# Streaming every product's moving operand as two interleaved halves, with the output put back in order on the host

## Chip, cores and metric

The kernel runs on one core of one Trainium2 chip. The metric is the device time of one execution in microseconds (us). Before the change it is 2234.18 us, the median of three runs that lie between 2234.03 and 2234.66 us.

## What is computed

A causal mixing over 7 tokens with softmaxed taps (one set of taps for each of 8 heads of 24 channels), and behind it a two-layer MLP with a squared ReLU. 8 x 4096 = 32768 tokens (S is 4096) of 192 channels each; the hidden layer has 2048 units.

```
w = softmax(weight, axis=-1)                       # 8 heads x 7 taps
x_pad = zeros(6 tokens) ++ x                       # per batch of 4096 tokens
attn[b, s, h*24:(h+1)*24] = sum_k w[h, k] * x_pad[b, s + k, h*24:(h+1)*24]
h = attn.reshape(32768, 192) @ w_in                # 192 -> 2048
r = maximum(h, 0)
out = (s * r * r + b) @ w_out                      # 2048 -> 192
```

## The kernel before, in words

**Layout.** Everything is kept transposed: channels or hidden units lie on the partitions, tokens along the free axis. A block is BLK = 512 tokens, so there are 64 blocks; two blocks make a unit that is loaded together. The output in memory is `outT`, 192 x 32768, and the host transposes it.

**Split operands.** Products are made in float32r (4 bytes an element, read in one pass). To keep precision each operand is held as a rounded high part and a low part, and three products stand for one: high x high, low weight x high, high weight x low. `sA`, `wA`, `tB` and `wB` are the two parts of the mixed tokens (`w...` are copies with the two halves of the partitions swapped); `W` and `WB` hold the split weights; `qh` and `ql` are the two parts of the squared hidden layer.

**First layer, `first` (L522, product at L531).** For a block and a pair `p` of hidden groups (8 pairs of 2 x 128 units) it fills a PSUM tile `h` of 128 x 2 x 512 with 18 products. Each has 64 contraction rows and 512 columns of tokens. The rows of group 0 lie on partitions 0 to 63 and those of group 1 on partitions 64 to 127, so that two products, one in each half of the array, run side by side. The text calls such a couple a **slot** of TensorE.

**Between the layers.** ACT takes the ReLU (L545) and squares it (L552); DVE rounds it to `qh` (L554) and subtracts to get `ql` (L559). All of these work on 128 x 1024 elements.

**Second layer, `second` (L604, product at L614).** 20 products of 64 rows and 512 columns for each block and pair, again two side by side, accumulate into four PSUM tiles. In blocks 0 and 1 `second_whole` (L569, products at L576 to L583) does it with 10 products of the full 128 rows, each a slot of its own. `last` (L667) finishes the last pair of the last block with 10 full products (L673, L674, L686).

**Order.** In the body each step issues `first` of one pair and then `second` of the pair LAG = 2 steps back, so that the work of ACT and DVE on a pair lies beside products of others. PSUM holds two `h` tiles. The convolution of later blocks is done on DVE in pieces between the steps; in the head two blocks' convolution is done by products in full float32 (`conv_tensor`, L257), where one product in the code gives two instructions. The head also has warm-up products (L388) and two products with a negated identity (L230).

**The streamed operand.** A matmul names the output, the stationary operand (weights) and the moving operand, which is streamed through the array column by column. In all lines that the change touches the moving operand is a row of 512 adjacent float32r elements on each partition, such as `sA[j][r, 0, :]` or `qh[:, i, :]`, and the output is a row of 512 adjacent elements of one PSUM bank.

Of the kernel before, what the change touches and what calls it, by code (L numbers as in the profile page):

```python
# [17 lines left out]
P = 128  # L18
BLK = 512
# [18 lines left out]
def conv_attention_then_squared_relu_mlp(  # L38
# [23 lines left out]
    nc = tc.nc  # L62
    D, T = outT.shape
# [4 lines left out]
    NF = 2 * NPAIR  # L68
# [43 lines left out]
    def in_order(*engines):  # L112
# [4 lines left out]
        for e in engines:  # L117
            mine = [i for i in traced[start:] if i.engine == e.engine]
            for before, i in zip(mine, mine[1:]):
# [6 lines left out]
                    reason="in_order",  # L126
                )


    class Tokens:  # L130
        def __init__(self, n):
# [143 lines left out]
    def w_in(part, p, chunk, rows):  # L275
        return W[rows, p, part, chunk * P : (chunk + 1) * P]

    def w_outA(part, f, rows=slice(0, P)):
        return W[rows, f // 2, part, CI + f % 2 * P :][:, 0:P]

    def w_outB(f, rows=slice(0, P)):
        return WB[rows, f // 2, f % 2, :]
# [239 lines left out]
    def first(n, j, p, meanwhile=None):  # L522
        h = ps_h.tile([P, 2, BLK], F32, name="h")
        halves = [tok[n].half(j, i) for i in range(2)]

        def both(w, part, at, start, stop):

            for i in range(2):
                chunk = halves[i][at]
                rows = slice(i * HB, (i + 1) * HB)  # L530
                nc.tensor.matmul(  # L531
                    h[:, i, :], w_in(w, p, chunk[0], rows), chunk[part], start=start, stop=stop
                )

        for at in (0, 2, 1):
            both(0, 1, at, at == 0, False)
            both(0, 2, at, False, False)
            both(1, 1, at, False, at == 1)
            if meanwhile and at == 0:
                meanwhile()  # L540
        return h
# [22 lines left out]
    def accumulators(n, j, p):  # L564
        if p == 0:
            acc[n, j] = [ps_o.tile([P, BLK], F32, name=f"acc{k}") for k in (1, 2, 1, 2)[: 4 if n else 2]]
        return acc[n, j]

    def second_whole(n, j, p, qh, ql):  # L569


        a1, a2 = accumulators(n, j, p)
        for i in range(2):
            f = 2 * p + i
            st, sp = f == 0, f == NF - 1
            nc.tensor.matmul(a2, w_outB(f), qh[:, i, :], start=st, stop=False)  # L576
            nc.tensor.matmul(a2, w_outB(f), ql[:, i, :], start=False, stop=sp)  # L577
        for i in range(2):
            f = 2 * p + i
            st, sp = f == 0, f == NF - 1  # L580
            nc.tensor.matmul(a1, w_outA(1, f), qh[:, i, :], start=st, stop=False)  # L581
            nc.tensor.matmul(a1, w_outA(0, f), qh[:, i, :], start=False, stop=False)  # L582
            nc.tensor.matmul(a1, w_outA(0, f), ql[:, i, :], start=False, stop=sp)  # L583
        if p == NPAIR - 1:
            t0 = n * SUP + j * BLK
            oA = outs.tile([P, BLK], F32, name="oA")
            nc.vector.tensor_scalar(oA, a1, sb, None, op0=ALU.mult)
            oC = outs.tile([DB, BLK], F32, name="oC", bufs=1)
            nc.scalar.activation(oC, a2[DB:P, :], AF.Identity, scale=sb[DB:P])
            oB = outs.tile([P, BLK], F32, name="oB")[0:DB]  # L590
            nc.vector.scalar_tensor_tensor(
                oB, a2[0:DB, :], sb[0:DB], oC, op0=ALU.mult, op1=ALU.add
            )
            unbiased.append((oA, outT[0:P, t0 : t0 + BLK], 0))
            unbiased.append((oB, outT[P:D, t0 : t0 + BLK], 2))
            del acc[n, j]
# [7 lines left out]
    def second(n, j, p, qh, ql):  # L604
        if (n, j, p) == steps[-1]:
            return last(n, j, qh, ql)
        accs = accumulators(n, j, p)

        ends = [NF - 1, NF - 1 if (n, j) != steps[-1][:2] else NF - 3]

        def both(to, w, f, q, start=False, stop=False):
            for i in range(2):
                r = slice(i * HB, (i + 1) * HB)
                nc.tensor.matmul(  # L614
                    accs[to + 2 * i], w(f, r), q[r, f % 2, :],
                    start=start and f == 0, stop=stop and f == ends[i],
                )

        for f in (2 * p, 2 * p + 1):
            both(1, w_outB, f, qh, start=True)  # L620
            both(1, w_outB, f, ql, stop=True)
        for f in (2 * p, 2 * p + 1):
            both(0, loA, f, qh, start=True)
            both(0, hiA, f, qh)
            both(0, hiA, f, ql, stop=True)
        if p == NPAIR - 1:
            t0 = n * SUP + j * BLK
            early = (n, j) == (1, 0)

            o = {}  # L630
            for k, name in ((1, "oB"), (0, "oA")):
                o[k] = outs.tile([P, BLK], F32, name=name)
                o[k + 2] = outs.tile([P, BLK], F32, name=name + "2", bufs=1)
                nc.scalar.activation(
                    o[k], accs[k], AF.Identity, scale=sb, bias=0.0 if early else bias[:, k : k + 1]
                )
                nc.scalar.activation(o[k + 2], accs[k + 2], AF.Identity, scale=sb)  # L637
            nc.gpsimd.tensor_tensor(o[1], o[1], o[3], op=ALU.add)  # L638

            oC = outs.tile([DB, BLK], F32, name="oC", bufs=1)  # L640
            nc.sync.dma_start(oC, o[1][DB:P])
            nc.gpsimd.tensor_tensor(o[0], o[0], o[2], op=ALU.add)
            toA, toB = outT[0:P, t0 : t0 + BLK], outT[P:D, t0 : t0 + BLK]
            oB = o[1][0:DB] if early else oC
            if not early:
                nc.sync.dma_start(toA, o[0])
            nc.gpsimd.tensor_tensor(oB, oC, o[1][0:DB], op=ALU.add)
            if early:
                unbiased.extend(((o[0], toA, 0), (oB, toB, 2)))
            else:  # L650
                nc.sync.dma_start(toB, oB)
            del acc[n, j]

    def upper_sums(accs):

        uA = outs.tile([P, BLK], F32, name="oA2", bufs=1)
        uB = outs.tile([DB, BLK], F32, name="oC", bufs=1)
        nc.scalar.activation(
            uB, accs[3][DB:P], AF.Identity, scale=sb[DB:P], bias=bias[DB:P, 1:2]
        )  # L660
        nc.scalar.activation(uA, accs[2], AF.Identity, scale=sb, bias=bias[:, 0:1])
        nc.vector.scalar_tensor_tensor(
            uB, accs[3][0:DB], sb[0:DB], uB, op0=ALU.mult, op1=ALU.add
        )
        return uA, uB

    def last(n, j, qh, ql):  # L667

        accs = accumulators(n, j, NPAIR - 1)
        uA, uB = upper_sums(accs)  # L670
        t0 = n * SUP + j * BLK
        for f in (NF - 2, NF - 1):
            nc.tensor.matmul(accs[1], w_outB(f), qh[:, f % 2, :], start=False, stop=False)  # L673
            nc.tensor.matmul(accs[1], w_outB(f), ql[:, f % 2, :], start=False, stop=f == NF - 1)  # L674
        oB = outs.tile([P, BLK], F32, name="oB")[0:DB]
        nc.vector.scalar_tensor_tensor(  # L676
            oB, accs[1][0:DB], sb[0:DB], uB, op0=ALU.mult, op1=ALU.add
        )
        nc.vector.scalar_tensor_tensor(
            oB, accs[1][DB:P], sb[DB:P], oB, op0=ALU.mult, op1=ALU.add  # L680
        )
        nc.sync.dma_start(outT[P:D, t0 : t0 + BLK], oB)
        oA = outs.tile([P, BLK], F32, name="oA")
        for f in (NF - 2, NF - 1):
            for w, q in ((loA, qh), (hiA, qh), (hiA, ql)):
                nc.tensor.matmul(  # L686
                    accs[0], w(f, slice(0, P)), q[:, f % 2, :],
                    start=False, stop=f == NF - 1 and q is ql,
                )
        for k, e in enumerate((nc.scalar, nc.sync)):  # L690
            c = slice(k * BLK // 2, (k + 1) * BLK // 2)
            nc.vector.scalar_tensor_tensor(
                oA[:, c], accs[0][:, c], sb, uA[:, c], op0=ALU.mult, op1=ALU.add
            )
            e.dma_start(outT[0:P, t0 + c.start : t0 + c.stop], oA[:, c])
# [81 lines left out]
    for n, j, p in steps:  # L777
# [7 lines left out]
        with begun() if n == 1 else ExitStack():  # L785
            h = first(n, j, p)
# [62 lines left out]
```

## Time and profile before

| | |
|---|---|
| median of the runs | 2234.18 us |
| profiled execution, first to last instruction | 2232.1 us |
| TensorE (PE) busy | 2226.5 us, 19330 products |
| weight loads (PEld) busy | 1829.2 us |
| VectorE (DVE) busy | 1755.6 us |
| ScalarE (ACT) busy | 1284.7 us |
| GpSimd (POOL) busy | 317.2 us |
| granted TensorE clock | 1.000 |

The span is what the profiler saw between the first and the last instruction; what lies around it makes up the difference of some 2 us to the median. Products of a matmul stream overlap each other: the time of one in the profile (386 ns) is longer than the distance between starts, and busy time counts overlapped time once. So the rate of TensorE is read from how many products start in a window, not from the duration of one. Two products that lie side by side in the two halves of the array start together.

### The profile page before, as it was taken

To read this page: it belongs to the slowest core of one execution; us is meant where nothing else is said; L and a number is where in the kernel's file an instruction comes from. 1 tells how busy PE (TensorE), PEld (TensorE's weight loads), DVE (VectorE), ACT (ScalarE), POOL (GpSimd) and SP (SyncE) were. 2 spreads that over 40 slices of the span, in tenths; PEclk is the share of its full clock that TensorE was granted. 3 is DMA by queue.
4 is the path that set the end of the run, shared out by engine and by line. 5 is a ranking of instruction groups with operands and counts; after the bars stand their busy time and mean duration, and the time that the engine had idled before them with its cause. 6 is when DMAs were issued, how large, how long until landed. Compare 5 with 4: busy or idle time off the path is not lost.

```text
span 2232.1 us, 45079 instructions
## 1 busy us (share of the span) xinstructions
PE 2226.5 (100%) x19330; PEld 1829.2 (82%) x19330; DVE 1755.6 (79%) x1997; ACT 1284.7 (58%) x1408; POOL 317.2 (14%) x205
## 2 busy tenths in 40 slices
PE   9999999999999999999999999999999999999999
PEld 6788888888888888888888888888888888888887
DVE  9898778777787787777877878778777787787764
ACT  8755555655555556555555555555655555556554
POOL 0022101111111011110110111101101111011110
PEclk9999999999999999999999999999999999999999
DMA  5113112121121111211111111112121121111110
GB/s 180 39 39 91 39 44 62 51 56 44 44 58 53 53 44 46 55 53 53 44 53 49 54 53 53 49 43 62 51 55 44 44 58 53 53 44 42 45 39 17
DMA packets 46168, 117.51 MB, mean 53 GB/s; under 512 B 7760, under 2 KB 8016, under 8 KB 45968
## 3 DMA queue, kind: packets, MB, share of 16 engines
q1 hardware_dynamic: 45824, 114.50, 18.6%
q8 instruction: 151, 2.47, 0.5%
q14 instruction: 49, 0.40, 0.1%
q10 hardware_dynamic: 144, 0.13, 0.0%
HBM read 31.64 MB, written 25.17 MB: 25 GB/s over the span
## 4 chain that ended last, share of the span: by engine, by line
PE 99%; DVE 0%; ACT 0%; issue 0%; DVEq 0%; POOL 0%; POOLq 0%
PE acc L614 50%; PE h L531 47%; PE acc L257 1%; PE acc L576 0%; PE acc L577 0%; PE acc L583 0%; PE acc L582 0%; PE acc L581 0%; PE acc L388 0%; DVE ql L559 0%; DVE accA L163 0%; DVE qh L554 0%; ACT q L552 0%; ACT q L545 0%; DVE oB L676 0%; DVE tB L216 0%
## 5 line engine op out<-in xcount | busy, mean ns | idle before, releaser
L545 ACT ACTIVATE q<-h 128x1024 f32<-128x1024 f32 x512 | 525.6, 1026 | 903.4 <-PE h L531 901.1
L559 DVE TENSOR_TENSOR ql<-q,qh 128x1024 fp32r<-128x1024 f32 x512 | 657.5, 1284 | 55.2 <-ACT qh L554 2.6
L554 DVE CAST qh<-q 128x1024 fp32r<-128x1024 f32 x497 | 370.5, 745 | 396.2 <-ACT q L552 393.8
L614 PE MATMUL acc<-qh,W 64*128 64x512 f32 x3960 | 609.9, 386 | 0.0
L552 ACT ACTIVATE q<-q 128x1024 f32<-128x1024 f32 x512 | 543.5, 1061 | 16.0
L614 PEld LDWEIGHTS acc<-qh,W 64*128 64x128 f32 x3960 | 370.9, 184 | 78.0
L531 PE MATMUL h<-sA,W 64*128 64x512 f32 x3072 | 432.4, 387 | 0.0
L531 PE MATMUL h<-wA,W 64*128 64x512 f32 x3072 | 431.5, 386 | 0.0
L531 PE MATMUL h<-tB,W 64*128 64x512 f32 x1536 | 429.9, 386 | 0.0
L531 PE MATMUL h<-wB,W 64*128 64x512 f32 x1536 | 429.9, 386 | 0.0
L614 PE MATMUL acc<-ql,WB 64*128 64x512 f32 x1980 | 385.7, 386 | 0.1
L614 PE MATMUL acc<-qh,WB 64*128 64x512 f32 x1980 | 385.6, 386 | 0.0
L614 PE MATMUL acc<-ql,W 64*128 64x512 f32 x1980 | 385.4, 386 | 0.0
L638 POOL TENSOR_TENSOR oB<-oB,oB 128x512 f32<-128x512 f32 x61 | 114.9, 1884 | 1672.6 <-ACT oB L637 1672.6
L163 DVE SCALAR_TENSOR_TENSOR accA<-xA,tap,accA 128x512 f32<-128x512 f32 x378 | 340.5, 901 | 6.8
L531 PEld LDWEIGHTS h<-sA,W 64*128 64x128 f32 x3072 | 287.3, 184 | 62.9 <-issue 1.8
L531 PEld LDWEIGHTS h<-wA,W 64*128 64x128 f32 x3072 | 287.8, 184 | 60.5
L531 PEld LDWEIGHTS h<-tB,W 64*128 64x128 f32 x1536 | 282.6, 184 | 40.5 <-issue 0.2
L531 PEld LDWEIGHTS h<-wB,W 64*128 64x128 f32 x1536 | 282.5, 184 | 20.1
L614 PEld LDWEIGHTS acc<-ql,WB 64*128 64x128 f32 x1980 | 185.5, 184 | 39.7 <-DVE ql L559 0.8
L614 PEld LDWEIGHTS acc<-ql,W 64*128 64x128 f32 x1980 | 185.5, 184 | 39.0
L614 PEld LDWEIGHTS acc<-qh,WB 64*128 64x128 f32 x1980 | 185.5, 184 | 38.8
(115 smaller groups left out, 1037.2 us busy)
## 6 DMA issues: line engine op xcount, KB each, us to landing
wA<-sA SPq DMA_DIRECT2D x126, 256.0 KB, 3.6
outT<-oA SPq DMA_DIRECT2D x63, 256.0 KB, 2.0
wB<-tB SPq DMA_DIRECT2D x60, 256.0 KB, 3.4
xA<-in_xA SPq DMA_DIRECT2D x24, 515.0 KB, 3.6
xB<-in_xB SPq DMA_DIRECT2D x32, 259.0 KB, 2.6
oC<-oB SPq DMA_DIRECT2D x61, 128.0 KB, 2.2
outT<-oC SPq DMA_DIRECT2D x60, 128.0 KB, 2.3
words<-in_w SPq DMA_DIRECT2D x7, 768.0 KB, 6.4
```

The source lines that it names most:

```text
L163: nc.vector.scalar_tensor_tensor(acc, src, w[:, k : k + 1], acc, op0=ALU.mult, op1=ALU.add)
L257: nc.tensor.matmul(acc, diag[:, k, :], x[:, k : k + BLK], start=k == 0, stop=k == K - 1)
L531: nc.tensor.matmul(h[:, i, :], w_in(w, p, chunk[0], rows), chunk[part], start=start, stop=stop)
L545: nc.scalar.activation(q, h, AF.Relu)
L552: nc.scalar.activation(q, q, AF.Square)
L554: cast(qh, q)
L559: nc.vector.tensor_tensor(ql, q, qh.bitcast(F32), op=ALU.subtract)
L614: nc.tensor.matmul(accs[to + 2 * i], w(f, r), q[r, f % 2, :], start=start and f == 0, stop=stop and f == ends[i],)
L638: nc.gpsimd.tensor_tensor(o[1], o[1], o[3], op=ALU.add)
```

## The change

Each moving operand of the products in `first`, `second`, `second_whole` and `last` is passed through a view that reads its 512 columns in the order 0, 256, 1, 257, 2, 258, and so on. Nothing is copied: only the access pattern of the instruction differs, a dimension of 256 steps of one element outside and a dimension of 2 with a step of 256 elements (1024 bytes) inside. The PSUM tiles are written as before, 512 adjacent columns.

So the tokens of a block stand in interleaved order in `h`. The second layer reads `qh` and `ql`, which are in that order, through the same view again, so that column 4a + 2u + v of its output is token 256u + 128v + a of the block. ReLU, square, rounding and the scaled sums work element by element and don't depend on the order. The host puts each block's columns back in order; this is outside the device time.

The products of the head (L257, L388, L230) and the two small products for the bias keep their operands. The instructions of every engine, their tiles, shapes and order are the same before and after; only line numbers shift by four or five.

```diff
+    def folded(columns):
+
+        return columns.rearrange("p (a b) -> p b a", a=2)
...
                 nc.tensor.matmul(
-                    h[:, i, :], w_in(w, p, chunk[0], rows), chunk[part], start=start, stop=stop
+                    h[:, i, :], w_in(w, p, chunk[0], rows), folded(chunk[part]),
+                    start=start, stop=stop,
                 )
...
-            nc.tensor.matmul(a2, w_outB(f), qh[:, i, :], start=st, stop=False)
-            nc.tensor.matmul(a2, w_outB(f), ql[:, i, :], start=False, stop=sp)
+            nc.tensor.matmul(a2, w_outB(f), folded(qh[:, i, :]), start=st, stop=False)
+            nc.tensor.matmul(a2, w_outB(f), folded(ql[:, i, :]), start=False, stop=sp)
...
-            nc.tensor.matmul(a1, w_outA(1, f), qh[:, i, :], start=st, stop=False)
-            nc.tensor.matmul(a1, w_outA(0, f), qh[:, i, :], start=False, stop=False)
-            nc.tensor.matmul(a1, w_outA(0, f), ql[:, i, :], start=False, stop=sp)
+            nc.tensor.matmul(a1, w_outA(1, f), folded(qh[:, i, :]), start=st, stop=False)
+            nc.tensor.matmul(a1, w_outA(0, f), folded(qh[:, i, :]), start=False, stop=False)
+            nc.tensor.matmul(a1, w_outA(0, f), folded(ql[:, i, :]), start=False, stop=sp)
...
                 nc.tensor.matmul(
-                    accs[to + 2 * i], w(f, r), q[r, f % 2, :],
+                    accs[to + 2 * i], w(f, r), folded(q[r, f % 2, :]),
...
-            nc.tensor.matmul(accs[1], w_outB(f), qh[:, f % 2, :], start=False, stop=False)
-            nc.tensor.matmul(accs[1], w_outB(f), ql[:, f % 2, :], start=False, stop=f == NF - 1)
+            nc.tensor.matmul(accs[1], w_outB(f), folded(qh[:, f % 2, :]), start=False, stop=False)
+            nc.tensor.matmul(accs[1], w_outB(f), folded(ql[:, f % 2, :]), start=False, stop=f == NF - 1)
...
-                    accs[0], w(f, slice(0, P)), q[:, f % 2, :],
+                    accs[0], w(f, slice(0, P)), folded(q[:, f % 2, :]),
...
-    return np.ascontiguousarray(r.results[0]["outT"].T)
+    out = r.results[0]["outT"].reshape(D, T // BLK, P, 2, 2)
+    return np.ascontiguousarray(out.transpose(1, 3, 4, 2, 0)).reshape(T, D)
```

## The prediction

> **What bounds the kernel now.** First the page's busy times and its chain of waits, to see which engine sets the end.
>
> ```profile
> span 2232.1 us, 45079 instructions
> PE 2226.5 (100%) x19330; PEld 1829.2 (82%) x19330; DVE 1755.6 (79%) x1997; ACT 1284.7 (58%) x1408; POOL 317.2 (14%) x205
> PEclk9999999999999999999999999999999999999999
> PE 99%; DVE 0%; ACT 0%; issue 0%; DVEq 0%; POOL 0%; POOLq 0%
> ```
>
> 99% of the chain that ended last is TensorE (PE) itself, and its clock is granted in full throughout. A busy PE is not yet a PE at its peak, so I look next at who made it wait (the waits of PE alone) and at how many products start in a stretch (busy time by windows: one of the steady body, one from the first changed product to the last).
>
> ```profile
> PE acc L388 <- POOL xA L145: 1.0, 1, 1.0
> 1000.00:2000.00 1000.00, 1000.00 (x8826) 826.48 (x8824) 785.51 (x872) 565.01 (x609) 143.28 (x90) 1.00 0.19 50
> 17.49:2227.00 2209.51, 2209.43 (x19295) 1821.58 (x19295) 1740.64 (x1968) 1271.78 (x1378) 316.32 (x197) 1.00 0.19 51
> ```
>
> PE waited 1.0 us in the whole run, at the warm-up. In the body 8826 products start in 1000 us. They start in couples, one in each half of the array, so 4413 slots: **226.6 ns a slot** of 512 columns. The chain says the same (start, duration, line, count): 40 products, 20 slots, in 4.53 us.
>
> ```profile
> 133.36 4.53 PE acc L614 x40
> ```
>
> So PE streams back to back: about 2.26 columns per ns, each column one 4-byte element read on each partition. Nothing but the time of a slot sets the length of the program.
>
> **The change part by part.** No instruction is added, removed or moved on any engine, no wait is new, no byte more is moved; the output rows have their old shape, and the host's reordering is not device time. What changes is how a slot reads its moving operand: adjacent elements before, afterwards each element 1024 bytes away from the one read just before it. So the sum has one term: the number of slots times what a slot gains or loses. The groups of products:
>
> ```profile
> L531 PE MATMUL h<-sA,W 64*128 64x512 f32 x3072 | 432.4, 387 | 0.0
> L531 PE MATMUL h<-wA,W 64*128 64x512 f32 x3072 | 431.5, 386 | 0.0
> L531 PE MATMUL h<-tB,W 64*128 64x512 f32 x1536 | 429.9, 386 | 0.0
> L531 PE MATMUL h<-wB,W 64*128 64x512 f32 x1536 | 429.9, 386 | 0.0
> L614 PE MATMUL acc<-qh,W 64*128 64x512 f32 x3960 | 609.9, 386 | 0.0
> L614 PE MATMUL acc<-ql,WB 64*128 64x512 f32 x1980 | 385.7, 386 | 0.1
> L614 PE MATMUL acc<-qh,WB 64*128 64x512 f32 x1980 | 385.6, 386 | 0.0
> L614 PE MATMUL acc<-ql,W 64*128 64x512 f32 x1980 | 385.4, 386 | 0.0
> ...
> L576 PE MATMUL acc<-qh,WB 128*128 128x512 f32 x32 | 13.0, 407 | 0.0
> L577 PE MATMUL acc<-ql,WB 128*128 128x512 f32 x32 | 12.6, 395 | 0.0
> L583 PE MATMUL acc<-ql,W 128*128 128x512 f32 x32 | 12.5, 391 | 0.0
> L582 PE MATMUL acc<-qh,W 128*128 128x512 f32 x32 | 12.5, 390 | 0.0
> L581 PE MATMUL acc<-qh,W 128*128 128x512 f32 x32 | 12.5, 389 | 0.0
> ```
>
> L531: 9216 products, 4608 slots. L614: 9900, 4950 slots. L576 to L583: 160 full products, 160 slots. The last pair adds 10 full ones by the code (L673, L674, L686). Together **9728 slots**; at 226.6 ns they make 2204.4 us of the 2209.5 us between 17.49 and 2227.00. So at most 5.1 us of gaps lie in there that a slower PE could swallow, the 17.5 us ahead (L257, L388: not changed) and the 5.1 us behind stay, and almost every added ns on a slot shows in full: 0.1 ns a slot is 0.97 us.
>
> **What a slot will take.** The trace has no row of PE reading elements that aren't neighbours, so I bound it from both sides. Lower end: 226.6 ns, no cost. There is no gain to expect: the clock is full and the only waits are the 1.0 us and the 5.1 us of gaps. For the upper ends I use rows in which PE takes its columns more slowly. The full-float32 products of the head (L257) show as two instructions for each of 14 calls, each with the same 512 columns of 4 bytes; their weight loads come once per instruction:
>
> ```profile
> 13.53 0.19 PEld L257 LDWEIGHTS acc<-xA,q 128*128 128x128 f32 x1 [0.24 <-issue]
> 13.96 0.19 PEld L257 LDWEIGHTS acc<-xA,q 128*128 128x128 f32 x1 [0.24 <-issue]
> 14.39 0.19 PEld L257 LDWEIGHTS acc<-xA,q 128*128 128x128 f32 x1 [0.24 <-issue]
> ...
> L257 PE MATMUL acc<-xA,q 128*128 128x512 f32 x14 | 6.3, 592 | 0.0
> ```
>
> One such instruction every 0.43 us: 430 ns for 512 columns, half the column rate of the changed products; and a whole call takes 860 ns. So PE has a half-rate pace here, 430 ns, and twice today's slot is 453 ns. These are the two ends of "half rate"; 860 ns is the upper end beyond.
>
> Which of them? Two facts of the rows speak for a halved rate. The moving port is by far the fastest reader of the kernel: 2.26 elements per ns and partition, against 1024 elements in 745 ns (1.37 per ns) on DVE and in 1061 ns (0.97) on ACT, all reading neighbours:
>
> ```profile
> L554 DVE CAST qh<-q 128x1024 fp32r<-128x1024 f32 x497 | 370.5, 745 | 396.2 <-ACT q L552 393.8
> L552 ACT ACTIVATE q<-q 128x1024 f32<-128x1024 f32 x512 | 543.5, 1061 | 16.0
> ```
>
> A rate of twice the others' is most simply had by fetching two neighbours at a time, and the new order leaves no two neighbours next to each other; then each fetch yields one element and the slot is paced at half rate. That is an inference, not something a row shows. Against it stands the one read of elements that aren't neighbours, ACT's step of 8 bytes through the weight words:
>
> ```profile
> L304 ACT ACTIVATE t<-words 128x768 f32<-128x768 f32 x7 | 6.4, 909 | 0.0
> ...
> L178 ACT CAST sA<-accA 128x512 fp32r<-128x512 f32 x63 | 38.1, 605 | 10.4 <-DVE accA L163 10.4
> ```
>
> Between 605 ns for 512 and 1061 ns for 1024 elements, 768 would take 833 ns; it takes 909, 9% more. But ACT asks for less than half as many elements per ns, and 8 bytes are not 1024. I take half rate, in the middle between its two rows: (430 + 453.2) / 2 = 441.6 ns, 215.0 ns more a slot.
>
> [...]
>
> **The sum.** 9728 x 215.0 ns = 2091.5 us. 2232.1 + 2091.5 = 4323.6 us of span; the profiled span stands 2.1 us below the median of the runs (2234.18), so **4325.7 us, I say 4325**. Ends of this case: 430 ns gives 2232.1 + 1978.7 - 5.1 (gaps swallowed) + 2.1 = 4207.8; 453.2 ns gives 2232.1 + 2204.4 + 2.1 = 4438.6. Nothing else can become late: DVE needs 1755.6 us and ACT 1284.7 us for the same work and have twice the time; the transfers that feed and drain the blocks get twice the time as well. The shape of the program stays, stretched.
>
> **The rivals.**
> (1) *No cost; the other side.* Addresses are known ahead and a long stream can be fetched ahead, so the time of a single fetch needn't show; then a slot stays at 226.6 ns and the run at 2234 us (2229 to 2239). It decides at one point: whether the port can deliver 2.26 scattered elements per ns and partition. For it: PE's stream is regular, its starts are unshaken to 0.01 us over hundreds of us, and ACT's small step cost 9%. Against it: it asks of scattered reads a rate that even neighbours reach nowhere else here. [...]
> (2) *Between.* The port gives scattered elements at the rate at which the next fastest reader takes neighbours, DVE's 1.37 per ns: 512 in 372.5 ns, 145.9 ns more a slot, 1419 us, 3653 us in all. For it speaks only that rates needn't be whole fractions.
> (3) *Every fetch waits for the one before.* If fetches aren't overlapped at all, a quarter rate is the row at hand, 860 ns: 633.4 ns more a slot, 6162 us, 8396 us in all. [...]
> (4) *It isn't what it says*, for instance because the operand is copied into order first: no such instruction exists in the changed program, and DVE would need a 745 ns cast for each 1024 columns. I give it nothing of its own.
>
> **How the numbers follow.** Half rate 0.60; no cost 0.25; between 0.05; quarter rate or worse 0.09; a gain 0.01. The predicted time is the half-rate one. Half rate alone would give 4208 to 4439. With (1) at 0.25 a range that leaves it out holds at most 0.74, so it must reach from the foot of rival (1), 2229, to just above half rate's upper end, 4440: that holds 0.60 + 0.25 + 0.05 = 0.90, and only the quarter rate and a larger gain lie outside. About 0.2% (4.5 us) is what a measurement of this kernel can tell from no change. Faster by more 0.01 (no mechanism; the gaps total 5.1 us), within it 0.24 (rival 1, less a little for a cost of 0.5 ns a slot, which would already show), slower 0.75.
>
> **What will show it.** If half rate is right: the count of products in a 1000 us window falls from 8826 to about 4530, the chain's pieces of 40 products take 8.8 us instead of 4.53, the mean duration of the changed products goes from 386 to about 590 ns (the L257 rows, at 430 ns apart, show 592 against 386 at 226.6), L257 itself stays at 592 ns, the busy times of DVE and ACT stay within a few per cent, their shares fall to about 41% and 30%, and the granted clock stays 1.00. If all changed lines slow alike, it is the read; if L531 slows and L614 doesn't, or the other way, my reason is wrong, for both read the same pattern. It would also be wrong if PE began to wait for someone, if the slots of the full 128 rows (L576 to L583) changed by another factor than the couples, or if ACT or DVE got slower: then it is the memory that is short, not PE's port. And 8826 products in 1000 us, as now, would show rival (1).

## The result and the profile after

The changed kernel takes 2135.34 us (median of 4 runs, 2134.63 to 2135.72) against 2234.23 us before: ratio 0.9557, 95% interval 0.9543 to 0.957. It became 4.4% faster where twice the time was forecast.

The page of the changed kernel, its span and busy times, and its windows (stretch, length, busy us and count of each engine, granted clock, DMA) in the steady body:

```profile
span 2133.8 us, 45079 instructions
...
PE 2123.6 (100%) x19330; PEld 1861.5 (87%) x19330; DVE 1752.4 (82%) x1997; ACT 1290.1 (60%) x1408; POOL 316.6 (15%) x205
...
1000.00:2000.00 1000.00, 1000.00 (x9270) 883.49 (x9268) 821.19 (x916) 595.46 (x639) 148.53 (x93) 1.00 0.20 53
```

9270 products in 1000 us where 8826 stood before: 4635 slots, 215.7 ns each in place of 226.6. The work of DVE and ACT is the same (1752.4 and 1290.1 us against 1755.6 and 1284.7), the clock is 1.00 in both. The chain of waits agrees: 40 products in 4.32 us, before 4.53.

```profile
266.74 4.32 PE acc L619 x40
...
299.55 4.32 PE acc L619 x40
```

The groups (busy, mean ns of one) show that both layers gained alike, 377 ns where 386 stood, and that the head's float32 products, which the change leaves alone (L261, before L257), kept their 592 ns; the full-row products of the first blocks (L586, before L581) went from 389 to 380 ns:

```profile
L619 PE MATMUL acc<-qh,W 64*128 64x512 f32 x3960 | 591.7, 377 | 0.1
...
L535 PE MATMUL h<-sA,W 64*128 64x512 f32 x3072 | 417.9, 377 | 2.5 <-DVE W L341 1.6
...
L586 PE MATMUL acc<-qh,W 128*128 128x512 f32 x32 | 12.1, 380 | 0.0
...
L261 PE MATMUL acc<-xA,q 128*128 128x512 f32 x14 | 6.3, 592 | 0.0
```

So the time went out of every slot. 9728 slots x 10.9 ns would be 106 us by these windows; the spans differ by 98.3 us. Most of the rest is a new wait: a faster PE runs into DVE, chiefly in the head, where the weights are still being split. The chain that ended last has it too: it was PE at 99% before, and DVE holds 5% of it now, in the first 180 us.

```profile
PE 94%; DVE 5%; ACT 1%; issue 1%; DMA 0%; SPq 0%; DVEq 0%; ACTq 0%
```

The waits of PE (time in all, times, longest) and the windows of one head stretch, after and then before, with PE alone:

```profile
PE h L535 <- DVE W L341: 1.6, 2, 0.9
PE acc L619 <- DVE ql L564: 1.2, 2, 0.9
PE acc L392 <- POOL xA L149: 1.0, 1, 1.0
PE h L535 <- ACT q L550: 0.9, 1, 0.9
PE acc L582 <- DVE ql L564: 0.4, 1, 0.4
```

```profile
30.00:60.00 30.00, 28.04 (x194) 1.00 0.30 111
```

```profile
30.00:60.00 30.00, 30.00 (x199) 1.00 0.28 103
```

PE is idle 10.2 us of the span after (2133.8 - 2123.6) and 5.6 us before: 4.6 us of the missing 7.7 us are these waits. The remaining 3 us I have not located.

### The profile page after: what moved, and what is told of

It reads as the page before. It is cut to its first block, busy times and chain, and to the rows that moved or that the text cites. A ratio compares the mean times of both kernels' runs of the same rounds, so it can differ in the third digit from the quotient of the medians.

```text
span 2133.8 us, 45079 instructions
## 1 busy us (share of the span) xinstructions
PE 2123.6 (100%) x19330; PEld 1861.5 (87%) x19330; DVE 1752.4 (82%) x1997; ACT 1290.1 (60%) x1408; POOL 316.6 (15%) x205
## 4 chain that ended last, share of the span: by engine, by line
PE 94%; DVE 5%; ACT 1%; issue 1%; DMA 0%; SPq 0%; DVEq 0%; ACTq 0%
PE acc L619 49%; PE h L535 44%; DVE ql L564 1%; DVE accA L167 1%; DVE c L333 0%; DVE qh L559 0%; DVE t L319 0%; DVE W L339 0%; DVE words L498 0%; DVE t L316 0%; DVE W L341 0%; DVE t L312 0%; ACT q L550 0%; DVE c L332 0%; DMA xA<-in_xA 0%
## 5 line engine op out<-in xcount | busy, mean ns | idle before, releaser
L559 DVE CAST qh<-q 128x1024 fp32r<-128x1024 f32 x497 | 370.4, 745 | 303.2 <-PE acc L619 215.8
L619 PE MATMUL acc<-qh,W 64*128 64x512 f32 x3960 | 591.7, 377 | 0.1
L619 PEld LDWEIGHTS acc<-qh,W 64*128 64x128 f32 x3960 | 378.5, 187 | 50.2 <-ACT oA L642 0.4
L535 PE MATMUL h<-sA,W 64*128 64x512 f32 x3072 | 417.9, 377 | 2.5 <-DVE W L341 1.6
L535 PE MATMUL h<-wA,W 64*128 64x512 f32 x3072 | 416.7, 377 | 0.0
L535 PE MATMUL h<-wB,W 64*128 64x512 f32 x1536 | 413.8, 377 | 0.0
L535 PE MATMUL h<-tB,W 64*128 64x512 f32 x1536 | 413.7, 377 | 0.0
L619 PE MATMUL acc<-ql,WB 64*128 64x512 f32 x1980 | 378.1, 377 | 1.3 <-DVE ql L564 1.2
L619 PE MATMUL acc<-qh,WB 64*128 64x512 f32 x1980 | 378.3, 377 | 0.1
L619 PE MATMUL acc<-ql,W 64*128 64x512 f32 x1980 | 378.1, 376 | 0.0
L535 PEld LDWEIGHTS h<-wA,W 64*128 64x128 f32 x3072 | 293.5, 187 | 38.7
```

Source lines behind the costliest of these rows:

```text
L535: nc.tensor.matmul(h[:, i, :], w_in(w, p, chunk[0], rows), folded(chunk[part]), start=start, stop=stop,)
L559: cast(qh, q)
L619: nc.tensor.matmul(accs[to + 2 * i], w(f, r), folded(q[r, f % 2, :]), start=start and f == 0, stop=stop and f == ends[i],)
```

## The experiments

All slots below are 1000 us divided by half the products that start between 1000 and 2000 us, unless another row is shown. The slot before is 226.6 ns and the slot after 215.7. A line or group of 16 bytes is four adjacent columns, the first of them a multiple of four: a unit to tell the orders by, not a part of the memory that a trace shows. Each kernel was run once beside the kernel before (2233.8 to 2234.6 us) except where more is said.

**First round: what in the order helps?** Only the order of the streamed columns differs from the changed kernel.

```diff
-        return columns.rearrange("p (a b) -> p b a", a=2)
+        return columns.rearrange("p (x y c) -> p y x c", x=2, c=128)   # e1_runs128
+        return columns.rearrange("p (x y c) -> p y x c", x=2, c=2)     # e1_pairs
+        return columns.rearrange("p (a b) -> p b a", a=128)            # e1_step16
```

> The changed products read runs of 128 adjacent columns, in the order 0 to 127, 256 to 383, 128 to 255, 384 to 511; the host restores the order. Theory A (a plain run costs because one neighbour after the other is read; the loss of 226.6 - 215.8 = 10.8 ns a slot is shared by the 511 neighbour steps): 508 of 511 neighbour steps are left, so 226.6 ns a slot, 2234 us. Theory B (the form counts: a one-dimensional pattern costs a fixed 10.8 ns, any pattern of two or more dimensions does not): 215.8 ns, 2135 us. Theory C (the far jump itself helps, two places of the memory being read in turn): three jumps do nothing, 226.6 ns, 2234 us.

2234.55 us; the slot as before:

```profile
1000.00:2000.00 1000.00, 1000.00 (x8826) 1.00 0.19 51
```

A pattern of several dimensions is not what helps: theory B falls.

> The changed products read couples of neighbours, 0, 1, 256, 257, 2, 3, 258, 259 and so on; the host restores the order. Theory A (cost per neighbour step): 256 of 511 neighbour steps are left, 221.2 ns a slot, about 2186 us. Theory B (form of the pattern): 215.8 ns, 2135 us. Theory C (two far places read in turn): 215.8 ns, 2135 us.

3269.07 us, 333 ns a slot:

```profile
1000.00:2000.00 1000.00, 1000.00 (x6004) 1.00 0.12 34
```

No theory had this: neighbours in couples from two places are far slower than either plain rows (226.6 ns) or the alternate order (215.7 ns).

> The changed products read every fourth column, 0, 4, 8 and so on to 508, then 1, 5, 9: a step of 16 bytes, never two elements of one 16-byte group in succession, and no far jumps; the host restores the order. Theory A (cost per neighbour step): 215.8 ns a slot, 2135 us. Theory B (form): 215.8 ns, 2135 us. Theory C (two far places in turn): no far jumps, so 226.6 ns, 2234 us, or worse if a new line each time costs.

4501.46 us, 460 ns a slot:

```profile
1000.00:2000.00 1000.00, 1000.00 (x4350) 1.00 0.09 25
```

Here is the half rate of the forecast, which the change itself did not meet. Theory A, a cost of neighbours as such, falls. C allowed for a time above 2234 us here, but it had expected 215.8 ns of the couples above, which took 333: two far places read in turn are not enough to explain the gain.

The fourth kernel is the one before with its tiles shifted.

```diff
-GAP = 296
+GAP = 288
```

> The kernel before with all tiles behind the filler tile moved down by 32 bytes (GAP 288 in place of 296); plain runs of 512 columns as before. Theories A, B and C: 226.6 ns a slot, 2234 us. Theory D (a plain run costs because each row begins at a multiple of 2 KiB, as the weights' rows do too): the slot changes, by up to 10.8 ns either way.

2234.36 us, 8828 products in the window, 226.5 ns. Shifting the tiles behind the filler by 32 bytes changes nothing (226.6 ns unshifted): theory D falls.

**Second round: distance, number of places, step.**

```diff
+        return columns.rearrange("p (y x b) -> p y b x", x=2, b=128)   # e2_dist128
+        return columns.rearrange("p (y x b) -> p y b x", x=2, b=4)     # e2_dist4
+        return columns.rearrange("p (a b) -> p b a", a=4)              # e2_four
+        return columns.rearrange("p (a b) -> p b a", a=256)            # e2_step8
```

> The changed products read the columns alternately from two places 512 bytes apart instead of 1024: 0, 128, 1, 129 and so on, in two stretches of 256 columns; the host restores the order. Theory E (the two elements that PE takes in a step must lie in different parts of the memory, and 1024 bytes happen to do that): another distance may miss it, then about 460 ns a slot as with the step of 16 bytes, 4500 us. Theory F (PE keeps the few lines that it read last, so that going back and forth between two lines, using each up, is free, whatever their distance): 216 ns, 2135 us. [...]

> The changed products read alternately from two neighbouring groups of 16 bytes: 0, 4, 1, 5, 2, 6, 3, 7, then 8, 12 and so on; the host restores the order. Theory E (distance decides): about 460 ns a slot, 4500 us, since 16 bytes was slow in the plain step. Theory F (lines kept): 216 ns, 2135 us. [...]

2135.97 us and 2132.65 us, 9270 products in the window in both, the slot of the changed kernel to the digit. The window of the smaller distance:

```profile
1000.00:2000.00 1000.00, 1000.00 (x9270) 1.00 0.20 53
```

The distance between the two places doesn't matter at the three distances tried, 1024, 512 and 16 bytes: theory E falls. Nor does the number of stretches that the pattern's third dimension strings together show: 2 at 512 bytes and 64 at 16 bytes, 215.7 ns both times.

> The changed products read the columns from four places in turn: 0, 128, 256, 384, 1, 129 and so on, a pattern of two dimensions; the host restores the order. Theory E (distance; couples lie 512 bytes apart): as for the distance of 512 bytes. Theory F: 216 ns and 2135 us if four lines are kept, about 460 ns and 4500 us if only two are. [...]

2783.19 us, 283 ns, between F's two answers:

```profile
1000.00:2000.00 1000.00, 1000.00 (x7062) 1.00 0.15 41
```

> The changed products read every second column, 0, 2, 4 and so on to 510, then 1, 3, 5: a step of 8 bytes, two elements of each 16-byte line; the host restores the order. Theory E and F: two elements of the line follow each other, one line a step of PE, 216 to 227 ns, 2135 to 2234 us. Theory H (only elements that are direct neighbours are fetched together, all others one by one unless they alternate between far places): about 460 ns, 4500 us.

4415.84 us, 451 ns:

```profile
1000.00:2000.00 1000.00, 1000.00 (x4436) 1.00 0.09 25
```

Two successive elements in each 16-byte group, and half the rate all the same. F, which with E expected 216 to 227 ns, falls on this; H fits here, but not the distance of 16 bytes above, which is no far place and is fast (215.7 ns).

**Third round: whose loss is it, the product's or the column's?**

```diff
# e3_first_only: folded() in first only
-            nc.tensor.matmul(a2, w_outB(f), folded(qh[:, i, :]), start=st, stop=False)
+            nc.tensor.matmul(a2, w_outB(f), qh[:, i, :], start=st, stop=False)
...
# e3_m64, e3_n256, e3_n256_alt: the kernel before, first() changed
+                m = P if start or stop else HB                     # e3_m64
+                    h[0:m, i, :], w_in(w, p, chunk[0], rows)[:, 0:m], chunk[part], ...
+                m = BLK if start else BLK // 2                     # e3_n256
+                    h[:, i, 0:m], w_in(w, p, chunk[0], rows), chunk[part][:, 0:m], ...
+                    chunk[part][:, 0:m].rearrange("p (y x b) -> p y b x", x=2, b=4), ...   # e3_n256_alt
```

> Only the first layer's products (4608 of the 9728 slots) read interleaved, the second layer reads plain rows; the host restores the order. If the gain belongs to each product by itself: 216 ns a slot in the first layer, 226.6 ns in the second, 4608 x 10.6 ns = 49 us less than before, 2185 us. If it needs all products of the stream alike (for instance because a change from one kind of pattern to the other costs): nearer to 2234 us.

2196.09 us, 38 us less than before where 49 were expected. The timeline of TensorE (start, duration, line, count):

```profile
801.94 0.81 PE L535 MATMUL h<-sA,W 64*128 64x512 f32 x6
802.58 0.38 PE L535 MATMUL h<-tB,W 64*128 64x512 f32 x1
...
803.88 0.40 PE L619 MATMUL acc<-qh,WB 64*128 64x512 f32 x2
804.11 0.40 PE L619 MATMUL acc<-ql,WB 64*128 64x512 f32 x2
804.35 0.39 PE L619 MATMUL acc<-qh,WB 64*128 64x512 f32 x2
804.58 0.39 PE L619 MATMUL acc<-ql,WB 64*128 64x512 f32 x2
804.80 0.62 PE L619 MATMUL acc<-qh,W 64*128 64x512 f32 x4
```

Three interleaved slots take 0.64 us (213 ns each within the rounding of 0.01 us); the first plain slots behind them take 0.23, 0.24, 0.23 and 0.22 us. The gain belongs to each product by itself, but a plain product right behind interleaved ones costs some ns more than among its like. The window of the steady body has this in sum:

```profile
1000.00:2000.00 1000.00, 1000.00 (x8988) 1.00 0.19 52
```

4494 slots, 222.5 ns each, where 9 interleaved slots of 215.7 ns and 10 plain ones of 226.6 ns would make 221.4 ns on average. 1.1 ns on each of 9728 slots is about the 11 us that are missing from the 49; what makes it I can't say.

> The kernel before, with plain rows, but 14 of the 18 products of each first-layer step use 64 of their 128 weight columns (they leave out half of the hidden units' sums, so the output isn't the reference's). Theory L (the loss of 10.8 ns a slot comes from the weights that are read beside the stream): half the weights, half the loss, about 221 ns for these slots, 9728 slots of which 3584 gain 5 ns, 2215 us. Theories J (a fixed loss at the start of each plain row) and K (a loss that goes with the columns): 226.6 ns, 2234 us.

2253.47 us. Two slots of half the weights' columns (array tile 64*64) lie between these two rows, 0.47 us, 235 ns each where 226.6 ns stood before:

```profile
799.66 0.63 PE L532 MATMUL h<-sA,W 64*64 64x512 f32 x4
800.13 0.38 PE L532 MATMUL h<-tB,W 64*64 64x512 f32 x1
```

The run took 19 us more than the kernel before, where L expected 19 us less and J and K no change. So half the weights don't halve the loss. That speaks against L, though the other array tile is a change of its own.

> The kernel before, with plain rows, but 16 of the 18 products of each first-layer step read only 256 of the 512 columns (they leave out half of the tokens' sums, so the output isn't the reference's). [...] The whole run: 1797 us by J and L, 1770 us by K, or somewhat more where DVE with its 1755 us of work becomes the bound; what counts is the distance of the slots.

1863.69 us, where J and L expected 1797. That figure stands on a slot of 256 columns of 120 ns, which no run before this one shows; the slots of 512 columns give J 215.7 / 2 + 10.9 = 118.8 ns and K 226.6 / 2 = 113.3 ns, an estimate each. DVE's 1755 us of work (the kernel before) would fill 94% of the run, so only the slots count. Six plain slots of 256 columns (12 products) between the first of these rows and the last, 0.72 us, 120 ns each:

```profile
804.03 0.28 PE L532 MATMUL h<-tB,W 64*128 64x256 f32 x1
...
804.39 0.52 PE L532 MATMUL h<-wA,W 64*128 64x256 f32 x6
804.75 0.40 PE L615 MATMUL acc<-qh,WB 64*128 64x512 f32 x2
```

> As the run with 256 columns, but those short products read alternately from two groups of 16 bytes (0, 4, 1, 5, 2, 6, 3, 7, then 8 and on); the same sums are left out, and what is left of the first layer is in another order, so the output isn't the reference's. [...] If the interleaving only hides something that a plain row of 256 columns has not: the same as there. The whole run about 1750 to 1800 us, DVE's work being 1755 us.

1848.94 us, above the 1750 to 1800 expected; no run shows the slot that the lower end stands on. Six alternate slots of 256 columns in 0.67 us, 112 ns each:

```profile
805.56 0.27 PE L532 MATMUL h<-tB,W 64*128 64x256 f32 x1
...
805.90 0.50 PE L532 MATMUL h<-wA,W 64*128 64x256 f32 x6
806.23 0.40 PE L616 MATMUL acc<-qh,WB 64*128 64x512 f32 x2
```

With 256 columns the plain slot is 120 ns, near the 118.8 ns of a fixed loss, as J had it; K, a loss with the columns, would have 113.3 ns and falls. The alternate short slot isn't at the half of its 215.7 ns either, 107.9 ns, but at 112: the distance between the two orders is 8 ns with 256 columns and 10.9 ns with 512, which is nearer to a fixed loss than to one that halves.

**Fourth round: what must an order of columns have?**

```diff
+        return columns[:, 0 : BLK // 2].unsqueeze(2).to_broadcast([columns.shape[0], BLK // 2, 2])   # e4_twice
+        return columns.rearrange("p (y x b) -> p y b x", x=2, b=2)            # e4_dist2
+        return columns.rearrange("p (a b c) -> p c b a", a=2, c=2)            # e4_alt_step2
+        return columns.rearrange("p (y x b) -> p y b x", x=2, b=4)            # e4_dist4_timed
```

> All changed products read 0, 0, 1, 1, 2, 2 and so on to 255, 255: each element twice, no alternation between places, half as many bytes (the other half of the tokens is left out, so the output isn't the reference's). [...] Theory S (each product needs two different places, for two read paths that keep a line each): 226.6 ns, 2234 us.

2134.67 us, the fast slot (9270 products in the window). No alternation between places is needed: S in this form falls.

> All changed products read 0, 2, 1, 3, then 4, 6, 5, 7 and so on: the same lines of 16 bytes in the same order as a plain row, only the order inside a line changed; the host restores the order. [...] Theory S: one place, two elements of a path's line in succession as in a plain row: 226.6 ns, 2234 us.

2233.99 us, the slot of the plain row:

```profile
1000.00:2000.00 1000.00, 1000.00 (x8828) 1.00 0.19 50
```

> All changed products read two far places in turn, but every second element of each: 0, 256, 2, 258, 4, 260 and so on, then the odd columns; the host restores the order. Theory S with lines of 16 bytes: each path has two elements of a line in succession, as in a plain row, 226.6 ns, 2234 us. [...] If alternating between two places is enough by itself: 216 ns, 2135 us.

2234.45 us, the slot of the plain row, though two far places are read in turn: alternation isn't sufficient either. Nor do groups of 8 bytes sort the orders: here as with the step of 8 bytes no two columns of such a group follow each other, neither in the stream nor in every second element, and that step took 451 ns.

```profile
1000.00:2000.00 1000.00, 1000.00 (x8828) 1.00 0.19 51
```

> All changed products read alternately from two neighbouring groups of 16 bytes (0, 4, 1, 5, 2, 6, 3, 7, then 8 and on), once more, timed; the host restores the order. Slots of 216 ns as with the change; 2132 to 2136 us, a ratio of 0.955 to the kernel before, so as fast as the change within 0.2%.

2133.02 us (median of 4, 2132.26 to 2133.5), ratio 0.9547 to the kernel before, interval 0.9531 to 0.9563: the same gain as the change's, within the intervals of the two.

**Twelve orders side by side.** One count sorts them all: take every second element of the stream (positions 0, 2, 4 and so on; the odd positions give the same count) and count how many in succession lie in one group of four columns (16 bytes).

| order of columns | in succession in a group, every second element | slot, ns |
|---|---|---|
| 0, 256, 1, 257 (the change) | 0, 1, 2, 3: four | 215.7 |
| 0, 128, 1, 129 | four | 215.7 |
| 0, 4, 1, 5 | four | 215.7 |
| 0, 0, 1, 1 | four | 215.7 |
| 0, 1, 2, 3 (before) | 0, 2: two | 226.6 |
| runs of 128 | two | 226.6 |
| 0, 2, 1, 3 | 0, 1: two | 226.5 |
| 0, 256, 2, 258 | 0, 2: two | 226.5 |
| 0, 128, 256, 384, 1 | 0, 256, 1: one | 283 |
| 0, 1, 256, 257, 2 | 0, 256, 2: one | 333 |
| 0, 2, 4 | 0, 4, 8: one | 451 |
| 0, 4, 8 | 0, 8, 16: one | 460 |

The count was formed after these runs, and no order was run to test it that it had not been formed on. It sorts them, but how TensorE reads the stream no trace shows, and it does not say why the four orders of the last class differ from 283 to 460 ns.

**Fifth round: what is the fixed loss?** The kernel before, plain rows; only the way in which the first layer's weights are read changes.

```diff
+        at = min(chunk, 1) * P
+        return W[rows, p, part, at : at + 2 * P : 2]                              # e5_w_step2
+        return W[rows, p, part, chunk * P : chunk * P + 1].to_broadcast([HB, P])  # e5_w_same
```

> The kernel before, streamed rows plain, but the first layer's weights are read with a step of 8 bytes from an area of twice the size (other weights than the right ones, so the output isn't the reference's): 64 groups of 16 bytes in place of 32 for each of its 4608 slots. [...] Theory R (the loss is the start of the stream's own reading, and the weights have their own way): 226.6 ns, 2234 us.

2267.29 us: three first-layer slots between the first two rows in 0.70 us, 233 ns each, 7 ns more than before: more than R's 226.6 ns, and less than the 237 ns (an estimate, 226.6 + 10.8) that a second loss, for twice the groups of weights, would make by L. The busy times of the page stand below them:

```profile
804.35 0.92 PE L535 MATMUL h<-sA,W 64*128 64x512 f32 x6
805.05 0.39 PE L535 MATMUL h<-wB,W 64*128 64x512 f32 x1
805.11 0.57 PE L535 MATMUL h<-tB,W 64*128 64x512 f32 x2
...
PE 2260.0 (100%) x19330; PEld 2231.5 (98%) x19330; DVE 1756.0 (78%) x1997; ACT 1285.4 (57%) x1408; POOL 316.3 (14%) x205
```

Two things besides the stream changed here: the two products of a couple no longer start together (805.05 and 805.11), and the weight loads are busy for 98% of the span where they were for 82%. So this run can't say whether the 7 ns are lost in the stream's reading or at the weights.

> The kernel before, streamed rows plain, but the first layer's products read one weight column 128 times, by a step of 0 (every unit gets the same weights, so the output isn't the reference's): one group of 16 bytes in place of 32. Theory L (weights' lines read in the stream's place): no loss is left in the first layer, 216 ns, 2234 - 49 = 2185 us. Theory R: 226.6 ns, 2234 us.

2254.34 us, 20 us more than before, which is 4.4 ns on each of the 4608 slots, or 231 ns on average; the three between these rows took 0.70 us:

```profile
804.34 0.85 PE L534 MATMUL h<-sA,W 64*128 64x512 f32 x6
805.04 0.39 PE L534 MATMUL h<-tB,W 64*128 64x512 f32 x1
```

The weight loads are at 82% of the span here, as before. With one group of 16 bytes of weights in place of 32 the loss should have gone by L, and the slots grew instead: L falls. R's 226.6 ns isn't met either; how the weights are read does touch the slot of a plain row by some ns.

## Why the prediction was wrong, point by point

- **What bounds the kernel: right.** TensorE's slots set the time before and after, and the sum over 9728 slots stands. DVE and ACT took no part except ahead of 180 us, at a price of 4.6 us of waits.
- **The failing step, first half: "Lower end: 226.6 ns, no cost. There is no gain to expect: the clock is full and the only waits are the 1.0 us and the 5.1 us of gaps."** A slot without a wait was taken for a slot without a loss. A plain row lost 10.9 ns at every product (226.6 against 215.7 ns), and still 8 ns with half the columns (120 against 112 ns). The quoted rows of before held a hint: the float32 instructions of the head stand 430 ns apart for 512 columns, a pace of twice that would be 215 ns by estimate, and the plain float32r slot stood 11.6 ns above it. Had the forecast set that figure beside the row, the loss would have been in sight. Whether the float32 rows have a loss of their own no run tests.
- **The failing step, second half: "the new order leaves no two neighbours next to each other; then each fetch yields one element and the slot is paced at half rate".** The forecast judged an order by its successive elements, and the runs rule that out: orders without any two neighbours in succession took 215.7 ns (the change), 226.5 ns (0, 256, 2, 258) and 283 to 460 ns. What sorts all twelve orders is every second element: there the new order has four in a group of four columns, and the plain row two. That the reader works by this count is inferred from the twelve and not shown.
- **The half rate exists, but not where the forecast put it.** Steps of 16 and 8 bytes take 460 and 451 ns a slot and 4501 and 4416 us, near the forecast's 441.6 ns and its end of 453. That is luck as far as the mechanism goes: the forecast gave this price to every order without neighbours, and others of them took 215.7, 226.5 and 283 ns.
- **The rivals.** "No cost" was the nearest, but its point of decision (can the port deliver 2.26 scattered elements per ns) misses that the changed order delivers more, 512 in 215.7 ns or 2.37 per ns. Rates between (rival 2) exist, at 283 and 333 ns, in orders other than the change's. A gain had been given 0.01.
- **What was to show it.** L261 stayed at 592 ns, both layers changed alike, the full-row products too (380 against 389 ns), DVE and ACT kept their busy times: these signs came, and they place the effect in TensorE's reading of the stream. The 4530 products in 1000 us and the 8.8 us for 40 products did not come.

**Open:** what the 10.9 ns of a plain row are, and why the order of the columns takes them away. That they are the start of each product's reading (theory R) was only argued, and no run shows it. Shown is that they don't halve with the columns (8 ns with 256), don't shrink with fewer groups of weights (231 ns with one in place of 32, 226.6 before), and stay when the tiles move by 32 bytes (226.5 ns).

## What to carry to other kernels

Where TensorE streams float32r back to back, don't take a slot without a wait for a slot without a loss: a slot lost 5% here (226.6 against 215.7 ns) with no wait in any view. For float32r rows, read two groups of four columns in turn (0, 4, 1, 5, 2, 6, 3, 7): it costs no instruction, took 4.5% here (2133.02 us against 2234.42), and elementwise work between two products doesn't mind the order (DVE 1752.4 us busy with the change, 1755.6 before) as long as the output is put back. Don't stream float32r with a constant step of 8 or 16 bytes: it doubled the time (4416 and 4501 us against 2234).

## What the runs showed that I had not expected

- The pace of the float32r stream goes with the groups of four columns in every second element in all twelve orders, 215.7, 226.6 or 283 to 460 ns for four, two or one in succession in a group, and not with the distance between two places read in turn (16, 512 and 1024 bytes alike).
- Two 16-byte groups read in couples of neighbours (333 ns) are slower than the same groups read in turn, element by element (215.7 ns).
- A plain product behind interleaved ones takes up to 0.24 us, more than among plain ones (0.227 us).
- How weights are read touches the slot of a plain row: with a step of 8 bytes a slot takes 233 ns, and with one column read 128 times 231 ns on average.
